# Closing the first 64 slots of each bucket before the last batch is routed, in an attention and top-2 expert kernel

## The chip, the cores and the metric

The kernel runs on one core of one Trainium2 chip. The metric is the device time of one execution in microseconds (us), as the median of several runs. The core has five engines that each execute their own list of instructions in order: TensorE (PE, matmuls and transposes), VectorE (DVE), ScalarE (ACT), GpSimd (POOL) and SyncE (SP). POOL issues the gathers, scatters and most loads, SP the writes of the token rows.

## The reference

Inputs are q, k and v (4 batches, 8 heads, 768 positions, 64 wide), 8 memory keys and values per head, and the router's and the experts' weights. First chunked attention, then a router that sends each of the 3072 tokens to two of eight experts:

```python
for c in range(nc):                       # chunks of 32, 16 to the left, 8 to the right, 8 of memory
    scores = scale * np.matmul(q_c, k_full.transpose(0, 1, 3, 2))
    a = softmax(scores)
    out[:, :, c_start:c_end] = np.matmul(a, v_full)
x = out.transpose(0, 2, 1, 3).reshape(B * S, H * D)          # 3072 tokens x 512
noisy = x @ w_gate + np.log1p(np.exp(x @ w_noise)) * noise
top2, top2_w = two largest of noisy, softmax over the two
for e in range(8):
    h = np.maximum(x[mask] @ w1[e], 0.0)                     # 512 -> 1024
    out[mask] += top2_w[mask, k, None] * (h @ w2[e])         # 1024 -> 512
```

## The kernel before

**Attention.** Work goes by 16 pairs (`NPAIR`), four for each batch. The loop of line 576 is software pipelined: in turn i, PE transposes the probabilities of pair i-1 (`PT_pe`), DVE takes the maximum over pair i's scores (`max_dve`), copies the transposed probabilities (`PT_dve`) and subtracts (`sub_dve`, whose exp runs on ACT), PE multiplies pair i-1 by the values (`PV_pe`) and forms the scores of i+1 (`scores_pe`), DVE normalizes pair i-1 into the token rows (`mult_dve`), and PE transposes rows of pair i-2 for the router (`xT_pe`, copied by ACT). The order on each engine is the order in which the program writes the calls; no scheduler changes it.

**Routing.** When the four pairs of a batch are through, `begin_route(b)` forms the logits (`logits_pe`) and the steps s1 to s8 follow, spread over the next turns by `early_steps` and `late_steps`. s1 (ACT) and s1n give noisy logits; s1m, s2d, s2a, s2g, s2b find the two largest and a one-hot of the expert pair; s3 (PE) ranks the tokens within their pair; s4 computes the gates and writes the batch's rows to `x_rows` in device memory; s5 and s5b turn ranks into a one-hot `Rn`; s4b, s6 (PE) and s7 turn that into a table `tab` of token numbers by bucket and slot. s8 (POOL) adds the batch to `seen`, the counts that s3 starts from. The last batch runs its steps on DVE (`side`), the others run some on POOL.

**Buckets.** The 28 pairs of experts are 28 buckets (`NB`) of 128 slots (`CAP`). A token beyond slot 127 of its bucket goes to a spill tile of 32. `gidx` holds the table as row numbers.

**Experts.** `gather(p)` fetches the 128 rows of bucket p by an indirect DMA from POOL. `turn(p)` transposes them on PE, and DVE copies them to `xTb`. Expert e uses seven buckets, in a larger and a smaller part (`halves(e)`): four and three. `plan[e]` lists the buckets that are new for e: seven for expert 0, six for expert 1. `first` multiplies by W1 in eight blocks of 128 outputs, each with a PSUM tile `ps_h`, followed by a ReLU on ACT or DVE. `second` multiplies one bucket by W2, and the second expert of a bucket scatters the finished rows to the output. Between the buckets of `second`, PE transposes the next expert's buckets. For expert 0, `first` is done in three pieces, and after the first of them stands `find_spill`, a chain of DVE steps that finds the tokens of the spill tile.

Between the last batch's logits and the first gather lies the whole routing chain of that batch:

```python
        begin_route(B - 1)
        late_steps()
        ...
        for p in plan[0]:
            gather(p)
        for e in range(E):
            ...
            if e == 0:
                parts = [big[:2], big[2:], small]
```

Of the kernel before, what the change touches and what calls it, by code (L numbers as in the profile page):

```python
# [24 lines left out]
def kernel(  # L25
# [35 lines left out]
    GP = 2  # L61
# [15 lines left out]
    xd_part = dram_disjoint_views(xd, B + 2)  # L77
# [7 lines left out]
    def body():  # L85
# [4 lines left out]
        psT = actx.enter_context(tc.psum_pool(name="psT", bufs=3))  # L90
# [6 lines left out]
        NVB, NKB = 3, 4  # L97
        turn_of = [0, 1, 0, 2, 1, 0, 2, 1]
        vbufs = [ap_.tile([128, ncnk, 2 * GP, 2, D], BF16, name=f"vg{i}", bufs=1) for i in range(NVB)]
# [129 lines left out]
        seen = rp.tile([128, NB], BF16, name="seen")  # L229
        rank_all = rp.tile([128, NP], F32, name="rank_all")  # L230
# [141 lines left out]
        def route(b):  # L372
# [61 lines left out]
            def s3():  # L434
# [6 lines left out]
                if b > 0:  # L441
                    nc.tensor.matmul(out=ps_r, lhsT=onesb, rhs=seen.rearrange("p (o e) -> p o e", o=1).to_broadcast([128, BT, NB]),
                                     start=False, stop=True, skip_group_check=True)
                R["ps_r"] = ps_r

            def s4():
# [4 lines left out]
                nc.vector.tensor_tensor(out=xrows[b][:, :, XC:].bitcast(F32), in0=ge, in1=bc(gs, E), op=Alu.mult)  # L451
                lo = XC if b == B - 1 else 0
                write_rows(b, b, 0, BT, lo, ROW)
# [56 lines left out]
            if b < B - 1:  # L510
                return first_steps, ((), ()), ((), (s1m, s2a, s2g, s2b, s4b)), ((s3,), (s4, s5)), ((), (s5b, s6)), ((), (s7, s8))
            return first_steps, ((), (s1n, s1m, s2d, s2a, s2g, s2b, s4b, s3, s4, s5, s5b, s6, s7))
# [62 lines left out]
        NEAR = 5  # L575
        for i in range(NPAIR):
            if i >= 1:
                PT_pe(i - 1)
            max_dve(i)
            for n in ahead(i):  # L580
                qkT_pe(n)
            fresh = i >= 3 and (i - 3) % HP == HP - 1
            if fresh:
# [4 lines left out]
            sub_dve(i)  # L588
            if i == 0:
# [12 lines left out]
            if i < NPAIR - 1:  # L602
                late_steps()
            if i in (2, 3, 4):
                zero_v(2, i - 2)
            if i >= 1:
                mult_dve(i - 1)
                if i - 1 == NPAIR - 2:
                    write_rows(B, B - 1, 0, UB, 0, XC)
            if i >= 2:  # L610
# [17 lines left out]
            if i >= 4 and i % GP == 0 and i // GP + 2 < NG:  # L628
                load_v(i // GP + 2)
            if i == GP * (NG - 3) + 1:  # L630
                load_w1(0)
                load_w2(0)
                load_w1(1)
# [4 lines left out]
        late_steps()  # L638
        PV_pe(n)
        mult_dve(n)  # L640
        write_rows(B + 1, B - 1, UB, BT, 0, XC)
        early_steps()
        xT_pe(n)
        late_steps()
# [323 lines left out]
```

## Time and profile before

| | |
|---|---|
| time, median of 3 runs | 341.07 us (340.34 to 342.45) |
| the profiled execution | 340.9 us, span 339.2 us |
| mean granted clock of PE | 0.968 |
| PE busy | 295.1 us (87%), 3492 matmuls |
| DVE busy | 170.8 us (50%), 341 instructions |
| ACT busy | 132.5 us (39%), 232 instructions |
| POOL busy | 137.9 us (41%), 181 instructions |
| indirect gathers of 128 rows | 28, mean 1061 ns on POOL |

The span is the time from the first to the last instruction of the profiled execution; its own time holds 1.7 us more around it. A busy share says how long an engine had an instruction under way, not how much of the time it set the end. In a row of the timeline stand the start and the duration in us, the engine, the line of the kernel, the operation with what it writes and reads, and in brackets the idle time before it and what ended it. A line such as L692 is a line of the kernel before.

### The profile page before, as it was taken

How to read it: one execution, taken by the hardware profiler on the slowest of the kernel's cores; microseconds unless marked ns; L12 is line 12 of the kernel's file. 1: busy time of each engine (PE TensorE's matmuls, PEld its weight loads, DVE VectorE, ACT ScalarE, POOL GpSimd, SP SyncE). 2: the span in 40 equal slices, each digit the busy share in tenths (PEclk: the TensorE clock that was granted, in tenths of full speed). 3: DMA queues.
4: the chain of work that ended last, by engine and by line, in shares of the span. 5: the costliest groups of instructions: out<-in, count | busy, mean ns of one | idle time of the engine just before them, and what ended most of it. 6: DMA issues, size and time to landing. Idle time of an engine off the chain costs nothing.

```text
span 339.2 us, 8160 instructions
## 1 busy us (share of the span) xinstructions
PE 295.1 (87%) x3492; PEld 180.0 (53%) x3492; DVE 170.8 (50%) x341; ACT 132.5 (39%) x232; POOL 137.9 (41%) x181
## 2 busy tenths in 40 slices
PE   1687888898753859999999999999999999999990
PEld 1566676776542645548547545545545545545540
DVE  7788779889686653224224233224413424434430
ACT  7867888795430423343333323223123113103100
POOL 8878885392233686400062043034250132141161
PEclk9999999999985699999999999999999999999997
DMA  7999999999991379970059129518849227221031
GB/s 102 183 180 192 187 164 198 221 104 164 228 276 26 96 111 226 224 130 2 2 84 229 31 60 198 95 56 148 181 107 200 57 80 126 40 93 53 6 130 66
DMA packets 58407, 42.87 MB, mean 126 GB/s; under 512 B 32215, under 2 KB 51799, under 8 KB 58368
## 3 DMA queue, kind: packets, MB, share of 16 engines
q0 software_dynamic: 49808, 38.80, 68.9%
q1 hardware_dynamic: 8272, 3.44, 4.7%
q8 instruction: 29, 0.48, 0.5%
q10 hardware_dynamic: 288, 0.07, 0.1%
q14 instruction: 10, 0.08, 0.1%
HBM read 61.32 MB, written 10.65 MB: 212 GB/s over the span
## 4 chain that ended last, share of the span: by engine, by line
PE 54%; issue 16%; DVE 15%; ACT 6%; POOL 5%; DMA 1%; POOLq 0%; DVEq 0%
PE ps_h L746 23%; PE ps_y L754 19%; POOL out_dram L762 4%; ACT kd L261 3%; DVE vg L136 2%; DVE mx L298 2%; DVE sd L303 2%; PE p_t L691 2%; DVE xrow L343 2%; PE ps_o L330 2%; PE ps_o L326 2%; ACT xt L356 2%; ACT P L305 1%; ACT qT L253 1%; PE ps_s L285 1%
## 5 line engine op out<-in xcount | busy, mean ns | idle before, releaser
L746 PE MATMUL ps_h<-xTb,w1t 128*128 128x512 bf16 (+3 forms) x608 | 106.6, 325 | 2.0 <-DVE xTb L692 2.0
L754 PE MATMUL ps_y<-w2t,ht 128*128 128x512 bf16 x448 | 102.0, 379 | 0.0
L746 PEld LDWEIGHTS <-w1t 128*128 128x128 bf16 x864 | 64.1, 97 | 45.2 <-DVE xTb L692 1.6
L762 POOL DMA_INDIRECT out_dram<-acc,sidx x28 | 27.9, 995 | 139.2 <-DVE acc L761 135.0
L734 DVE TENSOR_SCALAR ht<-ps_h 128x416 bf16<-128x416 f32 (+2 forms) x64 | 39.9, 625 | 72.8 <-PE ps_h L746 72.8
L732 ACT ACTIVATE ht<-ps_h 128x416 bf16<-128x416 f32 (+2 forms) x72 | 37.9, 526 | 76.7 <-PE ps_h L746 72.4
L754 PEld LDWEIGHTS <-ht 128*128 128x128 bf16 x448 | 41.9, 98 | 46.6
L758 ACT ACTIVATE acc<-ps_y,meta 128x512 f32<-128x512 f32 x28 | 19.2, 687 | 69.3 <-PE ps_y L754 56.5
L746 PE MATMUL ps_h<-xTs,w1t 128*128 128x32 bf16 x256 | 45.4, 177 | 0.2 <-DVE xTs L707 0.2
L761 DVE SCALAR_TENSOR_TENSOR acc<-ps_y,meta,acc 128x512 f32<-128x512 f32 x28 | 21.0, 751 | 37.0 <-PE ps_y L754 37.0
L682 POOL DMA_INDIRECT xl<-x_rows,gidx x28 | 29.7, 1061 | 15.4 <-issue 6.1
L120 POOL DMA_DIRECT2D vg<-in_v_dram x34 | 25.3, 753 | 8.2 <-PE ps_s L290 3.4
L692 DVE COPY xTb<-p_t 128x512 bf16<-128x512 bf16 x28 | 11.7, 422 | 29.0 <-PE p_t L691 29.0
L261 ACT COPY kd<-p_t 64x768 bf16<-64x768 bf16 x32 | 25.2, 786 | 1.0 <-PE p_t L250 0.7
L250 PE MATMUL p_t<-identb,qg 128*64 128x128 bf16 x192 | 10.3, 245 | 8.2 <-DMA qg<-in_q_dram 6.3
L305 ACT ACTIVATE P<-sd 128x768 bf16<-128x768 f32 x16 | 13.5, 844 | 9.5 <-DVE sd L303 9.5
L356 ACT COPY xt<-p_x 128x768 bf16<-128x768 bf16 x16 | 12.8, 798 | 8.0 <-PE p_x L354 7.7
L343 DVE TENSOR_TENSOR xrow<-ps_o,rec 128x768 bf16<-128x768 f32 x16 | 15.3, 958 | 0.6
L326 PE MATMUL ps_o<-memv,PT 128*128 128x260 bf16 x96 | 13.7, 279 | 2.0 <-DVE PT L317 2.0
L298 DVE TENSOR_REDUCE mx<-ps_s 128x12 f32<-128x768 f32 x16 | 15.1, 941 | 0.6 <-PE ps_s L285 0.6
L303 DVE TENSOR_TENSOR sd<-ps_s,mx 128x768 f32<-128x768 f32 x16 | 15.2, 947 | 0.0
L253 ACT COPY qT<-p_t 128x768 bf16<-128x768 bf16 x16 | 12.8, 800 | 5.0 <-PE p_t L250 4.7
(146 smaller groups left out, 305.6 us busy)
## 6 DMA issues: line engine op xcount, KB each, us to landing
w1t<-in_moe_w_dram POOLq DMA_DIRECT2D x8, 1024.0 KB
w2t<-in_moe_w_dram POOLq DMA_DIRECT2D x8, 1024.0 KB
vg<-in_v_dram POOLq DMA_DIRECT2D x30, 168.0 KB
qg<-in_q_dram POOLq DMA_DIRECT2D x7, 384.0 KB
kg<-in_k_dram POOLq DMA_DIRECT2D x7, 384.0 KB
x_rows<-xrow SPq DMA_DIRECT2D x3, 792.0 KB
x_rows<-xrow SPq DMA_DIRECT2D x2, 384.0 KB
xl<-x_rows,gidx POOLq DMA_INDIRECT x28
```

The lines of the kernel that those rows point to most:

```text
L120: nc.gpsimd.dma_start(out=vg[p0 + j:p0 + j + nj, c:c + n, hd, :, :].rearrange("p c e d -> p c (e d)"), in_=bass.AP(v.tensor, v.offset + (g ...
L261: nc.scalar.copy(st[n]["kT"][hs, hh, :].rearrange("d (p j) -> d p j", j=SJ), st[n]["p_k"][hs].rearrange("d j p -> d p j"))
L298: nc.vector.tensor_reduce(out=mx, in_=st[n]["ps"], axis=AX, op=Alu.max)
L303: nc.vector.tensor_tensor(out=sd, in0=st[n]["ps"], in1=bc4(st[n]["mx"], CTX), op=Alu.subtract)
L343: nc.vector.tensor_tensor(out=xr.rearrange("p u (h d) -> p u h d", d=D), in0=po[:, :, :MD].rearrange("p u (h d) -> p u h d", d=D), in1=rec ...
L682: nc.gpsimd.indirect_dma_start(out=xl, out_offset=None, in_=xd, in_offset=bass.IndirectOffsetOnAxis(ap=gidx[:, p:p + 1], axis=0), bounds_c ...
L732: nc.scalar.activation(out=dst, in_=src, func=Act.Relu)
L734: nc.vector.tensor_scalar(out=dst, in0=src, scalar1=0.0, scalar2=None, op0=Alu.max)
L746: nc.tensor.matmul(out=ps_h[:, o:o + w], lhsT=w1t[:, kp, f * 128:(f + 1) * 128], rhs=rhs(kp), start=(kp == 0 and i == 0), stop=(kp == KP - ...
L754: nc.tensor.matmul(out=ps_y, lhsT=ht[:, f, j * CAP:(j + 1) * CAP], rhs=w2t[:, f, :], start=(f == 0), stop=(f == FB - 1))
L761: nc.vector.scalar_tensor_tensor(out=a, in0=ps_y, scalar=gate, in1=a, op0=Alu.mult, op1=Alu.add)
L762: nc.gpsimd.indirect_dma_start(out=out_part[p], out_offset=bass.IndirectOffsetOnAxis(ap=sidx[:, p:p + 1], axis=0), in_=a, in_offset=None, ...
```

## The change

Three batches out of four are routed before attention ends. The change closes ("seals") the first 64 slots (`HB`) of each bucket to the last batch: where the three batches have filled fewer, `unsealed` raises the count from which the last batch's ranks start, so that its tokens stand in slots 64 and up. The sealed half of the buckets of experts 0 and 1 can then be fetched and multiplied by W1 while the last batch is being routed.

- Batch 2's routing is taken out of `begin_route`. Its logits stand in turn 13 (`LATE`), its steps s1m to s4 in turn 14 after `mult_dve(13)`, and s3, s8, s5, s5b, s6, s7 in turn 15, ahead of `PT_dve(15)`. Then `gidx_s` is formed from its table.
- The rows of batch 2 are written after turn 12, its gates apart.
- After the last logits POOL issues 13 gathers of 64 rows. On PE stand, in this order: half transposes of expert 0's four buckets, four blocks of its half of W1, s3 of the last batch, four more blocks, s6, the other three buckets with eight blocks, expert 1's transposes and two blocks, the overflow count, three blocks, the small matmuls of `find_spill`, three blocks.
- Then the 13 buckets are gathered again, whole, and the second half of their slots is transposed and multiplied (`turn_half(..., 1, ...)`, `half_first(e, ht, 1, ...)`).
- Steps s4b of the last batch move from POOL to DVE. `ps_h` has three buffers instead of four, `ps_y` three instead of two, the gather tiles thirteen instead of eight. The loads of W1 and W2 are issued in the order W1(0), W1(1), W2(0), over three turns.

```diff
+    HB = CAP // 2
+    SEALED = (B - 1) * S
...
                 if b > 0:
+                    before = (seen,) if b < B - 1 else (seen, unsealed)
+                    for x, r in enumerate(before):
+                        nc.tensor.matmul(out=ps_r, lhsT=onesb, rhs=r..., start=False, stop=(x == len(before) - 1), ...)
...
             def s4b():
-                eng = nc.gpsimd
+                eng = side
...
+            def s9():
+                ps_c = psT.tile([128, NB], F32, name="ps_c", tag="tr")
+                nc.tensor.matmul(out=ps_c, lhsT=onesb, rhs=seen, start=True, stop=True)
+
+            def s10():
+                short = T("short", [128, NB])
+                nc.vector.tensor_scalar(out=short, in0=R["ps_c"], scalar1=float(HB), scalar2=-1.0 / 128, op0=Alu.min, op1=Alu.mult)
+                nc.vector.tensor_scalar(out=unsealed, in0=short, scalar1=HB / 128, scalar2=None, op0=Alu.add)
...
+        NEAR, LATE = 5, HP * (B - 1) + 1
         for i in range(NPAIR):
             if i >= 1:
                 PT_pe(i - 1)
+            if i == LATE:
+                xT_pe(i - 2)
+            if i == NPAIR - 1:
+                steps["s3"]()
+                steps["s8"]()
             max_dve(i)
...
             sub_dve(i)
+            if i == NPAIR - 1:
+                steps["s5"]()
+                steps["s5b"]()
...
                 scores_pe(i + 1)
+            if i == LATE:
+                logits_pe(B - 2)
+                begin, steps = route(B - 2)
+                begin()
+            if i == NPAIR - 1:
+                steps["s6"]()
...
                 mult_dve(i - 1)
+                if i - 1 == HP * (B - 1) - 1:
+                    write_rows(0, B - 2, 0, BT, 0, XC)
                 if i - 1 == NPAIR - 2:
+                    write_rows(2, B - 1, 0, UB, 0, XC)
+                    steps["s7"]()
+                    nc.vector.tensor_scalar(out=gidx_s, in0=tabs[(B - 2) % 2][:HB], ...)
+            if i == LATE + 1:
+                for nm in ("s1m", "s2a", "s2g", "s2b", "s4b", "s4"):
+                    steps[nm]()
...
+        def turn_half(ps, h, eng):
+            p_t = psX.tile([128, KP, CAP], BF16, name="p_t")
+            hs = slice(HB * h, HB * h + HB)
+            for x, p in enumerate(ps):
+                for kp in range(KP):
+                    nc.tensor.transpose(out=p_t[:, kp, HB * x:HB * x + HB], in_=xl[hs, kp * 64:(kp + 1) * 64].bitcast(BF16), identity=identb[hs, hs])
+            ...
+            (nc.scalar.copy or nc.vector.tensor_copy)(dst, src)
...
+        for e in range(2):
+            for p in plan[e]:
+                gather_sealed(p)
+        for nm in ("s1n", "s1m", "s2d", "s2a"):
+            steps[nm]()
+        steps["s2g"]()
+        steps["s2b"]()
+        for ps in pairs(big):
+            turn_half(ps, 0, nc.scalar)
+        block = half_first(0, hts[0], 0, (0,), False, nc.scalar)
+        for f in range(4):
+            block(f)
+        steps["s3"]()
+        for nm in ("s4", "s4b", "s5", "s5b"):
+            steps[nm]()
+        for f in range(4, FB):
+            block(f)
+        steps["s6"]()
+        steps["s7"]()
...
+        for ps in pairs(small):
+            turn_half(ps, 0, nc.scalar)
+        block = half_first(0, hts[0], 0, (1,), False, nc.scalar)
+        for f in range(FB):
+            block(f)
+        for ps in pairs(plan[1]):
+            turn_half(ps, 0, nc.scalar)
+        block = half_first(1, hts[1], 0, (0, 1), False, nc.scalar)
+        block(0)
+        block(1)
         # the overflow count: 25 small matmuls
...
         for p in plan[0]:
             gather(p)
+        for f in range(2, 5):
+            block(f)
+        s_gi, s_si = find_spill()
+        gather_spill(s_gi)
+        for f in range(5, FB):
+            block(f)
...
+        for p in plan[1]:
+            gather(p)
+        load_w2(1)
         for e in range(E):
             if e == 0:
+                for x, ps in enumerate((big, small)):
+                    for pq in pairs(ps):
+                        turn_half(pq, 1, nc.vector)
+                    if x:
+                        turn_spill()
+                    block = half_first(e, ht, 1, (x,), x == 1)
+                    for f in range(FB):
+                        block(f)
+            elif e == 1:
+                block = half_first(e, ht, 1, (0, 1), True)
+                for f in range(FB):
+                    block(f)
```

`half_first` is `first` over 64 columns of each bucket instead of 128, block by block, with a ReLU of its own for the spill columns.

More of the change, by code (lines that the diff above doesn't have):

```diff
@@ L441, in s3 @@
                 if b > 0:
[L442 to L443 removed]
+                    before = (seen,) if b < B - 1 else (seen, unsealed)
+                    for x, r in enumerate(before):
+                        nc.tensor.matmul(out=ps_r, lhsT=onesb, rhs=r.rearrange("p (o e) -> p o e", o=1).to_broadcast([128, BT, NB]),
+                                         start=False, stop=(x == len(before) - 1), skip_group_check=True)
                 R["ps_r"] = ps_r
@@ L863, in body @@
             nxt = list(plan[e + 1]) if e + 1 < E else []
-            for p in nxt:
-                gather(p)
+            if e > 0:
+                for p in nxt:
+                    gather(p)
             if e + 2 < E:
```

144 lines of the change are left out of this document (92 added, 52 removed).

## The prediction

> **What bounds the kernel now.** I read the page first, then busy time in windows of 10 us, then the timeline from 63 to 136 us, where the change works, and last the chain of waits behind it.
>
> ```profile
> span 339.2 us, 8160 instructions
> ```
> ```profile
> 100.00:110.00 10.00, 2.74 (x46) 2.13 (x44) 7.21 (x35) 0.24 (x1) 3.38 (x4) 0.50 0.28 77
> 110.00:120.00 10.00, 7.05 (x56) 5.10 (x56) 6.89 (x17) 3.64 (x12) 6.85 (x7) 0.70 0.29 81
> ```
>
> Behind the times stand busy times by engine with instruction counts, PE's granted clock, DMA share and GB/s. Attention ends near 99 us. Until TensorE (PE) runs without gaps from about 127 us to the end, it mostly waits; its clock falls to 0.50 here. No DMA or other engine bounds the rest: PE's order and time do. So the change is worth what it takes from the stretch between the last attention pairs and expert 0's first W2 product, plus what it takes out of expert 1's W1 stage. Two chains of the timeline carry the rest (start, us, engine, operation, idle time before it).
>
> ```profile
> 87.48 0.23 DVE L342 RECIPROCAL rec<-ps_o 128x12 f32<-128x12 f32 x1 [1.09 <-PE ps_o L330]
> ...
> 87.75 0.96 DVE L343 TENSOR_TENSOR xrow<-ps_o,rec 128x768 bf16<-128x768 f32 x1
> ...
> 88.62 0.95 DVE L298 TENSOR_REDUCE mx<-ps_s 128x12 f32<-128x768 f32 x1
> ...
> 90.16 0.56 DVE L317 COPY PT<-p_p 128x768 bf16<-128x768 bf16 x1 [0.59 <-PE p_p L312]
> ...
> 92.46 0.23 DVE L342 RECIPROCAL rec<-ps_o 128x12 f32<-128x12 f32 x1 [0.88 <-PE ps_o L330]
> ...
> 93.60 0.55 DVE L317 COPY PT<-p_p 128x768 bf16<-128x768 bf16 x1
> ...
> 99.48 0.18 ACT L384 COPY lg<-ps_l 128x48 f32<-128x48 f32 x1
> ...
> 100.21 0.20 DVE L392 TENSOR_TENSOR nl<-ns,nz_all 128x48 f32<-128x48 f32 x1
> ...
> 101.00 0.21 DVE L401 TENSOR_TENSOR gd<-nl,m 128x48 f32<-128x48 f32 x1
> ...
> 103.13 0.27 DVE L430 TENSOR_TENSOR oh<-two 128x192 bf16<-128x192 bf16 x1
> ...
> 104.32 0.33 DVE L459 TENSOR_TENSOR rk<-oh,ps_r 128x168 f32<-128x168 bf16 x1
> ...
> 105.04 1.07 DVE L465 TENSOR_SCALAR Rn<-ramp,rank_all 128x128 bf16<-128x128 bf16 x6
> ...
> 106.66 0.18 DVE L651 TENSOR_SCALAR gidx<-tab 128x28 int32<-128x28 f32 x1
> ```
>
> VectorE (DVE) serves pairs 14 and 15 with idle gaps of 1.09, 0.59 and 0.88 us; pair 15's P transpose copy (PT) starts at 93.60. Logits of the last batch end at 99.66 (99.48 + 0.18), its routing starts at 100.21, late because DVE was still on batch 2's list, and the gather indices are there at 106.84.
>
> **Step 1: batch 2's routing moves ahead of pair 15.** DVE executes in order. Its list s1m, s2a, s2b, s4 now stands between mult(13) and max(15), and s5, s5b between sub(15) and mult(14), with s7 and gidx_s before PT(15). The same lists for batch 1:
>
> ```profile
> 72.19 0.19 DVE L399 TENSOR_REDUCE m<-nl 128x6 f32<-128x48 f32 x1
> ...
> 73.84 0.23 DVE L342 RECIPROCAL rec<-ps_o 128x12 f32<-128x12 f32 x1
> ...
> 77.17 0.20 DVE L448 TENSOR_TENSOR ge<-ge,two 128x48 f32<-128x48 f32 x1
> ...
> 77.99 0.32 DVE L459 TENSOR_TENSOR rk<-oh,ps_r 128x168 f32<-128x168 bf16 x1
> ```
>
> First list: 73.84 - 72.19 = 1.65, and 77.99 - 77.17 = 0.82, together 2.47 us; max(15) goes from 88.62 to 91.1. From max(15) to PT(15) there were 4.98 us with 0.59 + 0.88 idle, so 3.51 of work. The idle goes: pair 14's products need 1.74 us after its PT (90.72 to 92.46) and DVE has sub(15) and the second list meanwhile. Second list, rk to the end of Rn: 106.11 - 104.32 = 1.79. Two more of 0.2 each (gidx's row). PT(15) starts at 91.1 + 3.51 + 1.79 + 0.4 = 96.8 instead of 93.60: **3.2 us late**. Queued behind it are PV(15), mult(15), the last transposes and logits: 6.06 us from PT(15) to 99.66 before, so logits end at 102.86. Routing starts then, 2.7 later than now, since DVE is free. Bounds: if the 1.09 gap fills too, 2.1 late; if none fills, 4.7.
>
> **Step 2: the sealed gathers on GpSimd (POOL).** 13 gathers of 64 rows start 0.6 us after gidx_s (106.84 to 107.45 now), at 97.4. No such gather is in the trace.
>
> ```profile
> 6.47 0.58 POOL L120 DMA_DIRECT2D vg<-in_v_dram  x1
> ...
> 107.45 1.18 POOL L682 DMA_INDIRECT xl<-x_rows,gidx  x1 [2.82 <-DVE ov L790]
> ...
> 110.51 0.61 PE L691 MATMUL p_t<-identb,xl 128*128 128x128 bf16 x4 [2.42 <-DMA xl<-x_rows,gidx]
> ...
> 112.93 1.65 POOL L682 DMA_INDIRECT xl<-x_rows,gidx  x1 [0.30 <-issue]
> ```
>
> Bounds for one: 0.58, a plain DMA of 20 short rows, and 1.65, the slowest 128-row gather, plus 0.30 between two. I take 0.8 + 0.3, between the plain one and the usual 1.01. Thirteen end at 111.7; the first data land 3.05 after issue (110.50 - 107.45), the thirteenth at 113.7. The 13 full gathers, the spill gather and three weight loads queue behind them.
>
> **Step 3: what PE puts ahead of batch 3's ranks.** s3, the rank matmuls, now stand behind two half transposes and four blocks of expert 0. The first copy out of PSUM on ScalarE (ACT) stands behind the exp that needs gd.
>
> ```profile
> 112.89 5.14 PE L746 MATMUL ps_h<-xTb,w1t 128*128 128x256 bf16 x32 [0.52 <-DVE xTb L692]
> ...
> 116.32 2.13 ACT L732 ACTIVATE ht<-ps_h 128x256 bf16<-128x256 f32 x5 [0.29 <-PE ps_h L746]
> ...
> 118.11 0.62 PE L691 MATMUL p_t<-identb,xl 128*128 128x128 bf16 x8
> ...
> 120.17 3.67 PE L746 MATMUL ps_h<-xTb,w1t 128*128 128x256 bf16 x32 [1.44 <-DVE xTb L692]
> ```
> ```profile
> L356 ACT COPY xt<-p_x 128x768 bf16<-128x768 bf16 x16 | 12.8, 798 | 8.0 <-PE p_x L354 7.7
> ...
> L732 ACT ACTIVATE ht<-ps_h 128x256 bf16<-128x256 f32 x12 | 4.6, 383 | 7.1 <-PE ps_h L746 6.9
> ...
> L692 DVE COPY xTb<-p_t 128x512 bf16<-128x512 bf16 x28 | 11.7, 422 | 29.0 <-PE p_t L691 29.0
> ```
>
> gd ends 1.0 after routing starts (101.21 - 100.21): 103.9; the exp, like lg's 0.18, ends at 104.1. A copy of 512 columns on ACT lies between 0.38 (256) and 0.80 (768): 0.59. Copy, transposes at the low clock (0.61), copy: blocks start at 106. At the low clock, four blocks take 3.3 us (relu four starts at 116.32, PE began at 112.89), at the full clock 4 x 0.46. PE has been almost idle since 102.9, so I take 3.3: 109.3. s3 0.5 (0.92 now, with other DVE work between): 109.8, where DVE had its input ready at 106.1. Ranks and Rn 1.79, then 0.73 to the indices (106.84 - 106.11): **112.4, 5.6 later than now**. Blocks four to seven run under Rn; PE passes s6 at 112.0. If the clock stays up, 1.4 less.
>
> **Step 4: PE's order up to expert 0's W2.** One p_t buffer serves all half transposes, so each pair costs transposes (0.4, half the row of eight), copy and 0.1 of hand-over: 1.08 on ACT, 0.92 on DVE (0.42). Pair and single of the small half: 1.8. Eight blocks of 192 columns at ACT's 0.38: 3.0. Three pairs of expert 1: 3.25. PE is at 120.05.
>
> ```profile
> 85.20 0.74 PE L365 MATMUL ps_l<-wgn,xt 128*128 128x16 bf16 x24 [0.55 <-ACT xt L356]
> ...
> 108.82 0.18 DVE L800 TENSOR_TENSOR srank<-srank,ps_s 128x24 f32<-128x24 f32 x1 [1.10 <-PE ps_s L797]
> ...
> 109.22 0.15 DVE L807 CAST partb<-part 128x1 bf16<-128x1 f32 x1
> ...
> 112.75 0.95 DVE L812 TENSOR_TENSOR sone<-ramp,srank 128x768 bf16<-128x768 bf16 x1
> ...
> 115.96 1.44 DVE L818 TENSOR_REDUCE sum<-where 128x32 bf16<-128x768 bf16 x1
> ```
> ```profile
> 127.27 5.99 PE ps_h L746 x63
> 133.26 1.74 PE ps_y L754 x8
> 135.00 0.22 PE p_t L691 x4
> ...
> 147.37 12.98 PE ps_h L746 x128
> ```
>
> A matmul of 512 columns takes 0.217 (1.74 / 8), the smallest 0.031 (0.74 / 24). An expert 1 half block has 256, 128 and 64 columns four times: 0.77. Two blocks: 121.6; the overflow count, 25 tiny ones, 0.8: 122.4. DVE then needs 0.55 (108.82 to 109.37) and 4.65 for the spill search (112.75 to 117.40): 127.6. PE's three blocks under it end at 124.7, so **PE stands 2.9 us**, in order, although the full gathers have landed. Three more blocks: 130.1. Then expert 0's second halves: two pairs 1.85, 3.67, small half and spill transposes 2.25, last blocks 32 x (0.081 + 0.025) = 3.4 (0.025 for the 32 columns: 5.99 / 32 less 384 columns). W2 of expert 0 starts at 141.3; now 133.26: **+8.0**.
>
> **Step 5: what comes back.** Expert 1's W1 stage is 12.98 now; with half its columns left it takes 32 x (0.193 + 0.025) = 7.0: **-6.0**. Six sets of four transposes between W2 products get 64 columns each, 0.22 to 0.12: -0.6. Four ps_h buffers become three: relus of 0.38 hide under the next block, so nothing; at worst one per expert shows, 8 x 0.38 = 3.0. The later experts do the same work. The second gather of 13 buckets moves rows twice but lands ten us before PE asks.
>
> Edits at nothing, with their cover: logits(2) and its ACT steps move up one pair, behind scores(14), and take PE's 0.74 before PT(13) instead of after it, with xT(11) gone ahead. Batch 2's row write leaves SP one pair after its last mult, some 15 us before the first sealed gather waits for it; its gates follow alone. The three weight loads keep their place behind batch 1's POOL steps. The matmul and two DVE ops for unsealed run while PE and ACT make the last logits. oht and ohp, on DVE now, stand before the rank multiply, which waits for s3 until 109.8 anyway; without that cover about 0.5. The spill columns' own relus, 16 small ones on DVE, run beside ACT's.
>
> Sum: 8.0 - 6.0 - 0.6 = **+1.4 us**. The profiled execution took 340.9 (span 339.2 and 1.7 around it), so 342.3; the median of the runs shown, 341.07, is 0.2 above it. That is no change within the 1% (3.4 us) that a measurement of this kernel can tell from nothing. I sum by where PE can go on, since the added work fits the idle time of 100 to 120 us, but its order, not its load, decides.
>
> **Rivals.**
> - *Starved gathers (slower).* One gather beside DVE's 0.95 us sone took 1.65 instead of 1.01. If DVE's routing lists do that to all sealed gathers, the pitch is 1.95: the thirteenth starts at 97.4 + 12 x 1.95 = 120.8 and lands at 123.9, where its transposes are due at 119.0: 4.9 later, 347.2. It decides from a pitch of 1.54. Against it: gathers beside other DVE work took 1.01 to 1.18.
> The Trainium skill, page "SBUF — State Buffer", section "Who interferes with whom", says that VectorE copies and tensor_scalars in a two-port mode keep GpSimd from writing descriptors until they end, but infers that tensor_tensor does not. The slow gather here stood beside a tensor_tensor, so the measurement goes further than the page; by the page alone only PT and Rn (0.55 and 1.07) would stall gathers, too little for this rival, and 342.3 stands.
> - *PE's load decides (faster).* If PE really never waits after its first block, its work from 106 (3.3 + 0.5 + 1.8 + 0.4 + 2.6 + 6.2 + 1.0 + 3.7 + 3.4 and about 3 of transposes) ends at 132: 9.3 less, 333.0. For it: the windows show PE 73% idle at 100 to 110. Against it: one p_t buffer and the spill search in PE's order.
> - *DVE's gaps take batch 2's lists whole (no change).* Routing starts as now: 2.7 less, 339.6. Against it: 4.66 us of lists against gaps of 2.56, one of which waits on PE still.
> - *The clock stays up (no change).* 340.9. Against it: it stands at 0.50 over all of 100 to 110 us, where PE is 27% busy.
>
> **Chances.** Forecast 0.48, own range 339.5 to 345.5, of which 0.12 above 344.5; starved 0.20; load 0.12; gaps 0.10; clock 0.10. Faster by over 1%: 0.12. Slower: 0.20 + 0.12 = 0.32. Within 1%: 0.56. The range runs from 338.0 (gaps and clock together, 338.2) to 347.5 (starved); it leaves out the load case and little else.
>
> **What would show it.** Right: max(15) starts some 2.5 us later, with no DVE idle before PT(15); rank matmuls start about 3 us after oh; PE waits about 3 us before the eight tiny spill matmuls; expert 1's W1 stage takes near 7. Wrong: sealed gathers at a pitch over 1.5; PE without a wait before the spill matmuls; logits ending before 101; the low clock absent at the first sealed block; expert 0's W2 starting before 137 or after 145.

## Result and the profile after

The changed kernel takes 353.98 us, the kernel before 341.76 beside it: a ratio of 1.034 (95% interval 1.028 to 1.041). Two later measurements of the same pair gave 1.042 (1.036 to 1.047, and 1.037 to 1.047), so 11 to 14 us are lost where I had forecast 342.3 and no change. One of the four executions here (358.78 us), two of `change_again` (358.1 and 360.69) and two of `route_first_again` (356.67 and 357.03) were slow ones at a lower granted clock; times in this document are medians of all executions, and without these the three medians are 353.2, 353.6 and 351.2 us. The profiled execution took 353.15 us.

The page's first row and the windows that answer to those of before:

```profile
span 351.2 us, 8581 instructions
```
```profile
100.00:110.00 10.00, 4.94 (x83) 3.87 (x81) 5.54 (x16) 3.18 (x7) 3.10 (x3) 0.84 0.57 138
110.00:120.00 10.00, 7.08 (x54) 5.38 (x53) 3.06 (x15) 3.69 (x9) 7.56 (x9) 0.59 0.27 57
```

PE's busy time from 100 to 120 us has only gone from 9.8 to 12.0: the idle stretch that the sealed rows were to fill is filled little, and it lasts longer. The timeline shows where each station of the prediction now lies, behind one row of the kernel before, its maximum of pair 14:

```profile
84.02 0.95 DVE L298 TENSOR_REDUCE mx<-ps_s 128x12 f32<-128x768 f32 x1
```

```profile
87.40 0.96 DVE L302 TENSOR_REDUCE mx<-ps_s 128x12 f32<-128x768 f32 x1 [0.45 <-PE ps_s L289]
...
92.16 0.19 DVE L403 TENSOR_REDUCE m<-nl 128x6 f32<-128x48 f32 x1
...
95.17 0.95 DVE L302 TENSOR_REDUCE mx<-ps_s 128x12 f32<-128x768 f32 x1
95.28 0.36 SPq L463 DMA_DIRECT2D x_rows<-gt  x1
...
98.05 1.48 PE L334 MATMUL ps_o<-vg,PT 128*32 128x256 bf16 x24
...
100.95 0.17 DVE L646 TENSOR_SCALAR gidx_s<-tab 64x28 int32<-64x28 f32 x1
101.28 0.56 DVE L321 COPY PT<-p_p 128x768 bf16<-128x768 bf16 x1 [0.16 <-PE p_p L316]
...
106.29 1.11 POOL L713 DMA_INDIRECT xl<-x_rows,gidx_s  x1 [9.29 <-issue]
...
107.17 0.18 ACT L388 COPY lg<-ps_l 128x48 f32<-128x48 f32 x1
...
109.70 0.39 PE L724 MATMUL p_t<-identb,xl 64*128 64x64 bf16 x4 [3.02 <-DMA xl<-x_rows,gidx_s]
...
114.18 3.57 PE L807 MATMUL ps_h<-xTb,w1t 128*128 128x256 bf16 x16 [0.67 <-ACT xTb L731]
...
118.48 0.33 DVE L469 TENSOR_TENSOR rk<-oh,ps_r 128x168 f32<-128x168 bf16 x1 [6.73 <-PE ps_r L448]
...
120.86 0.18 DVE L893 TENSOR_SCALAR gidx<-tab 128x28 int32<-128x28 f32 x1
```

Pair 14's maximum, ahead of anything that the change moved on DVE except one pair's logits, is already 3.4 us late (84.02 before). The sealed indices are ready at 101.12, yet the first sealed gather starts at 106.29. PE then waits for its rows. The chain of waits names what the gather waited for, and shows the rest (start, us, what):

```profile
95.28 9.97 DMA x_rows<-gt
...
132.27 0.87 DVE sone L930
133.16 0.96 DVE where L932
134.12 2.69 DVE sum L936 x2
137.05 2.44 PE ps_h L807 x36
...
150.70 1.67 PE ps_y L836 x7
152.37 0.22 PE p_t L724 x4
152.59 1.83 PE ps_y L836 x8
...
172.55 1.46 PE ps_y L836 x6
```

W2 of expert 0 starts at 150.70 instead of 133.26, 17.4 us late. The write of batch 2's gates, 24 KB, takes 9.97 us to land. It stands in SP's queue behind the write of batch 2's rows: the records of single transfers in the trace have its first piece at 100.51, and the rows, issued at 82.67, land at 103.64.

### The profile page after: what moved, and what is told of

It reads as the page before. It is cut to its first block, busy times and chain, and to the rows that moved or that the text cites. A ratio compares the mean times of both kernels' runs of the same rounds, so it can differ in the third digit from the quotient of the medians.

```text
span 351.2 us, 8581 instructions
## 1 busy us (share of the span) xinstructions
PE 300.6 (86%) x3656; PEld 188.6 (54%) x3674; DVE 166.0 (47%) x347; ACT 143.8 (41%) x259; POOL 149.3 (43%) x192
## 4 chain that ended last, share of the span: by engine, by line
PE 66%; DVE 13%; ACT 7%; issue 6%; DMA 4%; POOL 2%; POOLq 0%; DVEq 0%
PE ps_y L836 25%; PE ps_h L828 22%; PE ps_h L807 7%; DMA x_rows<-gt 3%; ACT kd L265 2%; DVE vg L139 2%; PE ps_o L334 2%; DVE mx L302 2%; PE ps_o L330 2%; DVE xrow L347 2%; DVE sd L307 2%; POOL out_dram L844 2%; ACT xt L360 1%; PE p_t L724 1%; PE p_t L254 1%
## 5 line engine op out<-in xcount | busy, mean ns | idle before, releaser
L836 PE MATMUL ps_y<-w2t,ht 128*128 128x512 bf16 x430 | 99.9, 379 | 1.6 <-issue 1.0
L828 PE MATMUL ps_h<-xTb,w1t 128*128 128x512 bf16 (+3 forms) x416 | 78.4, 336 | 0.0
L788 ACT ACTIVATE ht<-ps_h 128x512 bf16<-128x512 f32 (+4 forms) x92 | 45.4, 493 | 75.2 <-PE ps_h L828 54.9
L790 DVE TENSOR_SCALAR ht<-ps_h 128x512 bf16<-128x512 f32 (+3 forms) x68 | 35.6, 523 | 68.6 <-PE ps_h L828 55.7
L828 PEld LDWEIGHTS <-w1t 128*128 128x128 bf16 x608 | 44.4, 96 | 34.7
L828 PE MATMUL ps_h<-xTs,w1t 128*128 128x32 bf16 x192 | 34.1, 177 | 0.0
L807 PE MATMUL ps_h<-xTb,w1t 128*128 128x128 bf16 (+3 forms) x320 | 31.0, 254 | 2.1 <-ACT xTb L731 1.6
L807 PEld LDWEIGHTS <-w1t 128*128 128x128 bf16 x320 | 26.2, 102 | 5.7 <-issue 2.0
L713 POOL DMA_INDIRECT xl<-x_rows,gidx_s x13 | 12.9, 990 | 12.9 <-issue 12.6
L330 PE MATMUL ps_o<-memv,PT 128*128 128x260 bf16 x96 | 14.7, 293 | 3.2 <-DVE PT L321 3.2
```

The source lines that it names most:

```text
L330: nc.tensor.matmul(out=po[:, u, :OW], lhsT=PT[:, 2 * u + e, :], rhs=memv[:, g, e, :], start=(e == 0), stop=False, skip_group_check=True)
L788: nc.scalar.activation(out=dst, in_=src, func=Act.Relu)
L790: nc.vector.tensor_scalar(out=dst, in0=src, scalar1=0.0, scalar2=None, op0=Alu.max)
L807: nc.tensor.matmul(out=ps_h[:, o:o + w], lhsT=lhsT, rhs=xTv[:, kp, z[0]:z[-1] + 1:(z[1] - z[0] if len(z) > 1 else 1), hs], start=(kp == 0 ...
L828: nc.tensor.matmul(out=ps_h[:, o:o + w], lhsT=w1t[:, kp, f * 128:(f + 1) * 128], rhs=rhs(kp), start=(kp == 0 and i == 0), stop=(kp == KP - ...
L836: nc.tensor.matmul(out=ps_y, lhsT=ht[:, f, j * CAP:(j + 1) * CAP], rhs=w2t[:, f, :], start=(f == 0), stop=(f == FB - 1))
```

## The experiments

They ran in five groups, each on one chip with the kernel before beside it, which took 344.3, 342.4, 342.6, 341.2 and 341.4 us. I compare within a group, or by ratio. The diffs are shortened, and where the order is all that changes, they name steps instead of quoting every line.

**1. Four single edits, in a bad moment.** `late_gates` issues batch 2's gate write behind the sealed gathers:

```diff
-                    nc.sync.dma_start(out=xd_part[b - (B - 2)]..., in_=gt.bitcast(I32))   # in s4
+        gate_rows(0, B - 2, late_gates)                    # behind the 13 gather_sealed
```

> Edit: the gate write of batch 2 is issued behind the sealed gathers instead of ahead of them (the gate columns of its rows hold zeros until then; no sealed gather's gate columns are used). Theory 1 (the first sealed gather waits 4.6 us for this write to land, 106.29 against gidx_s at 101.12): the first sealed gather starts some 0.6 us after gidx_s, at about 101.7; no transpose of a sealed row waits for a gather any more, the first four cold blocks start at about 111 instead of 114.2, W2 of expert 0 at about 147 instead of 150.7, and the time is 349 to 350.5 us, 3 to 4.5 below the change. Rival A (the weights' traffic starves the gathers themselves): they are issued at 101.7, but their pitch goes from 1.27 us to over 1.8 and they land later than 5 us after issue while the weights arrive; the blocks start no earlier than 113 and the time stays above 352. Rival B (PE is held by something else there): the gathers are early, the blocks still start at 114, no gain.

`w2_later`:

```diff
-            if i == GP * (NG - 3) + 2:
-                load_w2(0)
+        load_w2(0)                                         # behind the 13 gather_sealed
```

> Edit: W2 of expert 0 (1 MB) is loaded behind the sealed gathers instead of at turn 12. Theory 1a (the gate write's 768 pieces of 32 bytes need 9.97 us because they stand behind 3 MB of weights and the rows, which arrive at 240 GB/s until about 102): 1 MB less is some 4.4 us less, the write lands at about 101, the first sealed gather starts within 1 us of gidx_s, and the time falls by 3 to 4.5 us against the change, as in the run beside it. Rival C (the write takes 10 us by itself, its pieces are small): it lands some 10 us after its issue as before, the first sealed gather starts at about 106, and the time stays at 352 to 354. In both, W2 of expert 0 lands by about 130, ahead of its first use at about 147.

`route_first`:

```diff
+        steps["s3"](); s4, s4b, s5, s5b
         for f in range(4):
             block(f)
-        steps["s3"](); s4, s4b, s5, s5b
+        steps["s6"]()
         for f in range(4, FB):
             block(f)
-        steps["s6"]()
```

> Edit: the last batch's rank matmuls go to PE ahead of the four cold blocks and its index matmuls behind them (the change has them 4 and 8 blocks later). Theory 2 (the indices' lateness, 120.9 against 106.7 before, is not what sets the end: POOL is busy with sealed gathers until 122.8 and the first full gather's rows are used at 139.5): gidx comes 3 to 4 us earlier, the first full gather stays at about 123, PE's wait ahead of the spill sums falls by 0 to 1 us, the time stays within 1 us of the change (352.2 to 354). Rival D (the ranks and the indices are on the path, as the term of 5.6 us in the sum has it): the spill search and W2 of expert 0 come 3 us earlier, the time falls to about 350.

`early_search`:

```diff
+        overflow count; for p in plan[0]: gather(p)       # right behind gidx
         small half: turn_half, eight blocks; turn_half(expert 1)
+        s_gi, s_si = find_spill(); gather_spill(s_gi)
         block = half_first(1, hts[1], 0, (0, 1), False, nc.scalar)
```

> Edit: the overflow count is put right behind the last indices, and the spill search ahead of expert 1's first block (the change has them behind two and five of its blocks). Theory 3 (PE stands about 3 us ahead of the spill sums, waiting for DVE's list of 5.2 us behind the overflow count): that wait goes, expert 1's blocks run through, W2 of expert 0 starts at about 147.7 instead of 150.7, the time is 350 to 351. Rival E (something else ends that wait, the full gathers or the spill's gather): the second halves of expert 0 wait for rows instead, W2 of expert 0 stays after 149.5 and the time above 352.

Measured: 379.7, 378.1, 375.9 and 381.1 us, ratios 1.105, 1.095, 1.093 and 1.105, all 22 to 27 us longer than the change. Their traces hold stands that nothing explains, as ACT's second sealed copy in `route_first`, 4.6 us after its transposes had ended:

```profile
110.31 0.39 PE L724 MATMUL p_t<-identb,xl 64*128 64x64 bf16 x4 [0.45 <-DMA xl<-x_rows,gidx_s]
...
115.30 0.59 ACT L731 COPY xTb<-p_t 128x512 bf16<-128x512 bf16 x1 [5.86 <-remote]
```

So the times decide nothing yet; two rows do. In `late_gates` the gate write is out of the way and the first gather is still late, and in `w2_later` it is on time (one fence each):

```profile
103.99 0.17 DVE L653 TENSOR_SCALAR gidx_s<-tab 64x28 int32<-64x28 f32 x1
...
108.31 1.11 POOL L721 DMA_INDIRECT xl<-x_rows,gidx_s  x1 [8.28 <-DVE unsealed L532]
```
```profile
101.45 0.17 DVE L646 TENSOR_SCALAR gidx_s<-tab 64x28 int32<-64x28 f32 x1
...
102.06 1.10 POOL L711 DMA_INDIRECT xl<-x_rows,gidx_s  x1 [4.57 <-DVE gidx_s L646]
```

The name in the first bracket only ended close to the gather's start; the gather doesn't need it, since in `aligned_w2_later` below it starts 4 us ahead of `unsealed`. The gather's own waits in the program are three row writes, the gate write, an older load and the index. In `late_gates` the rows of batch 2 were issued at 84.48 and landed at 107.36, 0.95 us ahead of the gather. So not the gate write alone: the rows, issued some 20 us ahead of the index, are late too as long as 3 MB of weights are under way. `w2_later` needs no gate edit to be on time. Two things remained open: the stands, and what made attention late.

**2. The change again, and two edits.** `change_again` and `before_again` are the two kernels unchanged; the latter, run once, took 340.7 us.

> The changed kernel once more, unaltered, beside the edits of this call: in the first four runs each edit gave 373 to 380 us where the change had been 353, with DVE, ACT and PE standing 2.4 to 6.5 us at a time between 107 and 171 us for nothing that a row of theirs names. Theory F (these stands are a delivery of instructions or descriptors that comes late while many small transfers run, and vary with the chip or the moment): the change itself comes out at 370 to 380 here, with the same stands. Rival G (each of the four edits brought them on): the change stays at 352 to 355 and stands nowhere over 1.5 us in that stretch.

`gates_and_search` has the edits of `late_gates` and `early_search` together; `expert0_only` leaves expert 1's sealed gathers, transposes and eight blocks out of the stretch, and expert 1 runs its W1 whole, as before:

```diff
-        for e in range(2):
-            for p in plan[e]:
-                gather_sealed(p)
+        for p in plan[0]:
+            gather_sealed(p)
...
-            elif e == 1:
-                half_first(e, ht, 1, (0, 1), True), eight blocks
```

> Edit: both the gate write of batch 2 behind the sealed gathers and the spill search ahead of expert 1's blocks. Theories 1 and 3 (4.6 us of wait for the gate write, 3 us of PE's wait ahead of the spill sums, both on the path): 5 to 7.5 us below the change in the same call. Rival (other stands take their place): less than 2 us below it.

> Edit: only expert 0's buckets are gathered sealed and multiplied ahead; expert 1's six sealed gathers, its turns and its eight blocks ahead are gone and it is treated as the experts behind it. Theory 4 (expert 1's 11 us ahead, 128.3 to 139.5 with the wait in it, and 3.2 of turns cost more than the 6 us that its stage saves): W2 of expert 0 starts 8 us earlier than in the change, expert 1's W1 stage is 13 instead of 7, the time is 1 to 3 us below the change in the same call. With theory F on top, fewer small transfers are fewer stands: up to 10 us below it. Rival H (PE stood idle anyway until the full gathers have landed, so that the work ahead of expert 1 is free): 4 to 6 us above the change.

Measured: 356.6 (1.042), 370.4 (1.081) and 355.6 us (1.040, interval 1.037 to 1.044). No stands this time, and the change repeats.

`gates_and_search` has a flaw of mine, the same as `early_search`: the full gathers stand in POOL's order ahead of transposes that I had left behind them, and these now read the full gathers' rows. Its timeline:

```profile
125.73 0.95 SPq L557 DMA_DIRECT2D x_rows<-gt  x2
...
129.04 1.04 POOL L745 DMA_INDIRECT xl<-x_rows,gidx  x1 [5.13 <-DMA x_rows<-gt]
...
137.22 0.39 PE L732 MATMUL p_t<-identb,xl 64*128 64x64 bf16 x4 [12.89 <-DMA xl<-x_rows,gidx]
```

So both kernels say nothing on the search. The first row does say something: batch 2's gate write, the first of its two, issued at 125.73 when no weights move, has landed at 127.70 by the trace, 2.0 us later, not 9.97. `expert0_only` reaches W2 of expert 0 at 145.90, 3.8 us earlier than `change_again` (149.74) where I had expected 8, and pays it back with 12.98 us of W1 for expert 1, where the change needs 7.0. Expert 1's share of the change is worth nothing that these times can tell.

**3. Places of the tiles.** The change adds small tiles ahead of `qg`, `kg`, `vg` and the weights, which moves all of them 832 bytes on, from a multiple of 256 to one plus 64. `before_shifted` does that to the kernel before, with an unused tile; `aligned` takes it back in the change:

```diff
     wp = ctx.enter_context(tc.tile_pool(name="wp", bufs=1))
+    filler = rt.tile([128, 16], F32, name="filler", bufs=1)     # before_shifted: 64 bytes
+    filler = rt.tile([128, 48], F32, name="filler", bufs=1)     # aligned: 192 bytes
```

> Edit: the kernel before with 64 bytes of filler at that place, nothing else: its tiles now lie as the change's do, 64 bytes behind a multiple of 256. Theory 5: 256-byte pieces take 44 ns and over, the maximum of turn 14 comes at 86 to 87.5 instead of 84.0 to 84.6, the time is 2 to 4 us above the kernel before. Rival J: 41 to 42 ns, no difference beyond 1 us.

> Edit: the change with 192 bytes of filler per partition ahead of the weights' tiles, nothing else. In the kernel before, the tiles of the weights and of the q, k and v loads began at addresses that are multiples of 256 bytes; the change's new small tiles and buffer counts push all of them 832 bytes on, to 64 behind such a multiple, and the filler takes them to a multiple again. In the transfer records the 256-byte pieces of those loads take 41 ns in the kernel before and 44 to 59 ns in the change and every edit of it. Theory 5 (that shift slows the loads of the attention stage, PE's instructions come later behind them, 1.0 to 1.2 us at turns 8 and 9): 256-byte pieces back at 41 to 42 ns, the maximum of turn 14 at 84.0 to 84.8 instead of 86.7 to 87.4, and the time 2 to 3.5 us below the change (349 to 352 where it has 353 to 356). Rival J (the pieces are slow for another reason, the order of the v buffers or the traffic of that chip): 44 ns and over, turn 14 at 86 or later, no gain.

`aligned_w2_later` adds the edit of `w2_later`; `aligned_w2_search` adds to that the early search with the full gathers behind all sealed transposes:

> Edit: the filler, and W2 of expert 0 loaded behind the sealed gathers. Theory 1a (with 1 MB less ahead of them, the rows and gates of batch 2 have landed when the sealed indices are ready): the first sealed gather starts 0.6 us after gidx_s, the first four cold blocks start at 109 to 110 with the gather landing some 2.6 us after issue, W2 of expert 0 at 143 to 144, and the time is 4 to 5.5 us below the filler alone. Rival (PE then waits elsewhere): less than 2 us below it. In the first run with this edit the stage from 107 to 160 held stands of 2 to 10 us that no row explains; should they be here too, they belong to the tiles' place or to that edit, and not to the moment.

> Edit: as the run before, and the spill search ahead of expert 1's blocks, its first part right behind the last indices (this time the full gathers stay behind the turns of the sealed rows; in the two earlier runs with this edit the turns of the three buckets of the small half read the full gathers' rows and PE waited 12.9 us for them). Theory 3: PE's wait of about 2.5 us ahead of the spill sums goes, W2 of expert 0 starts 2.5 to 3 us earlier than in the run before, at about 141, the time is 2 to 3 us below it, near the kernel before. Rival E: another wait takes its place, less than 1 us.

Measured: `before_shifted` 344.12, ratio 1.0046 (1.0006 to 1.0087); `aligned` 352.71, 1.030 (1.020 to 1.039); `aligned_w2_later` 348.89, 1.016 (1.009 to 1.024); `aligned_w2_search` 347.63, 1.013 (1.006 to 1.020).

An unused tile of 64 bytes costs the kernel before 1.6 us; the interval allows 0.2 to 3.0, and I had expected 2 to 4. The profile shows how: the DMA part of the pages of `before_again` and of `before_shifted` have the same packets and bytes in the queue of loads, at another share of the time,

```profile
q0 software_dynamic: 49808, 38.80, 69.0%
```
```profile
q0 software_dynamic: 49808, 38.80, 72.2%
```

and turn 14's maximum, with the longest stand of PE ahead of it, in the timelines of the two:

```profile
84.61 0.95 DVE L298 TENSOR_REDUCE mx<-ps_s 128x12 f32<-128x768 f32 x1
```
```profile
56.88 0.50 PE L286 MATMUL ps_s<-kd,qT 128*32 128x112 bf16 x20 [2.19 <-issue]
...
87.41 0.95 DVE L299 TENSOR_REDUCE mx<-ps_s 128x12 f32<-128x768 f32 x1
```

Over all profiled executions this maximum starts at 84.0 to 86.7 in the eight with aligned tiles (median 84.8), at 85.8 to 91.5 in the twelve with shifted ones (median 88.3). Three of the eight stand at 86.3 to 86.7, so the place of the tiles is not all that moves it. The records of single transfers separate the two without an overlap: 21,492 pieces of 256 bytes take 41.3 to 41.5 ns on average in the eight, 45.4 to 54.2 in the twelve. The median piece takes 41 in all; 0.4 to 0.6% against 5 to 13% take over 80. For the change itself the time alone doesn't separate it: the interval of `aligned` overlaps the change's.

The weights are the larger part. W2 of expert 0 moved behind the gathers is worth 3.8 us beside `aligned`, with all four executions of the one below all four of the other. DMA in windows of 2 us (last column GB/s), first of `aligned`, whose index was ready at 98.20 and whose first gather started at 103.31, then of `aligned_w2_later`, 100.08 and 100.36:

```profile
98.00:100.00 2.00, 1.63 (x32) 1.38 (x36) 0.63 (x3) 1.12 (x2) 0.00 (x0) 1.00 1.22 237
100.00:102.00 2.00, 0.77 (x22) 0.47 (x12) 1.46 (x4) 0.00 (x0) 0.00 (x0) 1.00 0.55 135
```
```profile
98.00:100.00 2.00, 2.00 (x36) 1.59 (x26) 1.48 (x5) 0.41 (x1) 0.00 (x0) 0.50 0.00 0
100.00:102.00 2.00, 1.75 (x14) 1.26 (x12) 0.63 (x2) 1.11 (x2) 1.33 (x2) 0.61 0.55 197
```

The traces also hold when each write landed, which the gather waits for (us):

| | change | `late_gates` | `aligned` | `aligned_w2_later` |
|---|---|---|---|---|
| rows of batch 2, issued | 82.67 | 84.48 | 80.67 | 82.54 |
| rows of batch 2, landed | 103.64 | 107.36 | 100.80 | 98.09 |
| gates of batch 2, landed | 105.25 | behind the gathers | 102.27 | 98.55 |
| last piece of W2 of expert 0 | 104.5 | 108.6 | 101.5 | behind the gathers |
| sealed index ready | 101.12 | 104.16 | 98.20 | 100.08 |
| first sealed gather | 106.29 | 108.31 | 103.31 | 100.36 |

With W2 ahead of the gathers, the writes land about when it does, and the gather starts 0.95 to 1.04 us behind the last of them; with W2 behind the gathers, both writes are there before the index. The gather doesn't wait for the load itself: in `late_gates` it starts before W2's last piece. The search ahead of expert 1's blocks gains 1.3 us, less than the 2.5 us that PE had stood there, and inside the intervals. In `aligned_w2_search` another wait shows: the transposes of the second pair wait for the first copy on ACT, which stands behind the last batch's exp.

```profile
107.25 0.59 ACT L730 COPY xTb<-p_t 128x512 bf16<-128x512 bf16 x1
...
107.89 0.37 PE L723 MATMUL p_t<-identb,xl 64*128 64x64 bf16 x4 [2.26 <-ACT xTb L730]
```

**4. What is left, aligned.** All three start from `aligned_w2_search` or its parts. `sealed_copy_first` puts the first copy ahead of the exp:

```diff
-        for nm in ("s1n", "s1m", "s2d", "s2a"): ...
+        for nm in ("s1n", "s1m", "s2d"): ...
+        turn_half(pairs(big)[0], 0, nc.scalar)
+        s2a, s2g, s2b
```

> Edit: on top of the filler, the later W2 load and the early spill search, ACT's first copy of sealed rows goes ahead of the last batch's exponential (L423 there), nothing else. Theory 6 (with the gathers early, the first transposes end at 105.6 and their copy stands on ACT until 107.25 behind that exponential, which waits for the routing list on DVE; PE waits 2.26 us for the copy's buffer): the copy starts at about 105.7, PE's wait falls below 0.8, the first blocks start at 108.3 to 108.8 instead of 109.7, the time is 1 to 1.5 us below aligned_w2_search. Rival K (the third and fourth gathers land no earlier, 108.6): the blocks start at 109.3 or later, less than 0.5 us.

`route_first_aligned` adds the edit of `route_first` to `aligned_w2_search`, `expert0_only_aligned` that of `expert0_only` to `aligned_w2_later`; `change_third` is the change.

> Edit: on top of the filler, the later W2 load and the early spill search, the last batch's rank and index matmuls go 4 and 8 blocks ahead as in route_first. Theory 2: the indices come 3 us earlier, the first full gather stays behind POOL's sealed gathers at about 117.5, the time stays within 1 us of aligned_w2_search (347.6). Rival D: 2 us or more below it. If stands of 2 us and more that no row explains appear between 107 and 160 us, as in route_first, they go with this edit; if not, they went with that moment.

> Edit: the filler and the later W2 load, and expert 1's sealed gathers, turns and eight blocks ahead left out as in expert0_only. Theory 4, corrected by that run (W2 of expert 0 came 3.8 us earlier there though its attention stage had been 2.3 us slower, and expert 1's stage took 13 instead of 7): what expert 1's work costs ahead, 6 us, is what it saves behind, so the time is within 1.5 us of aligned_w2_later (348.9). Rival H: 4 to 6 us above it. Rival L (less low clock and fewer transfers make it the better kernel): 2 us or more below it.

Measured: 346.07 (1.015, 1.011 to 1.019), 346.25 (1.012, 1.005 to 1.019), 347.92 (1.020, 1.014 to 1.026), and the change 355.11 beside them. In the change's profile of this group the index comes at 103.28, the gates land at 104.59 and the first sealed gather starts at 105.63, 2.3 us behind the index where I had expected 4.5 to 5.3. The repairs of `sealed_copy_first` together give 9.0 us of the change's 13.9 back. PE's wait for the first copy falls to 0.96:

```profile
105.50 0.27 PE L723 MATMUL p_t<-identb,xl 64*128 64x64 bf16 x4 [0.96 <-ACT xTb L730]
...
108.55 3.57 PE L806 MATMUL ps_h<-xTb,w1t 128*128 128x256 bf16 x16 [0.67 <-ACT xTb L730]
```

The wait for the next rows grows to 1.71, so part of the gain goes there. The three kernels lie within 1.9 us of each other, so the copy, the place of the rank matmuls and expert 1's early half can't be told apart by the time. None beats the kernel before.

**5. Two of the first group again.**

> The edit of w2_later once more (W2 of expert 0 behind the sealed gathers, tiles where the change has them). If the stands of 2.4 to 10.6 us on ACT, DVE and PE in its first run belonged to the moment: none over 1.5 us after 100 us, the first sealed gather 0.5 us behind gidx_s, the time 3 to 5 us below the change's 353 to 356, so 349 to 352. If they belong to the edit: 370 and over with the same stands.

> The edit of route_first once more (the last batch's rank and index matmuls 4 and 8 blocks ahead, tiles where the change has them). Moment: no stands, 352 to 356, within 1.5 us of the change. Edit: 370 and over, ACT at the second sealed copy and at the first block's result 4 to 6 us late again.

`w2_later` takes 351.17 (1.025, 1.017 to 1.033, where the change had 1.034 to 1.042) instead of 378.1, `route_first` 354.37 (1.026, 1.017 to 1.036) instead of 375.9. So the 22 to 27 us of the first group belonged to its moment, not to these two edits; the other two were not run again alone. The interval of `route_first` overlaps the change's, so its edit can't be told from none. The chip alone did not bring the stands either, since the second group ran on the same one and the change had no such stands there. The kernel before took 344.3 beside them. What the stands were stays open.

## Why the prediction was wrong

The prediction's way, leg by leg, in the profiled executions (us; `repaired` is `sealed_copy_first`):

| | before | predicted | change | repaired |
|---|---|---|---|---|
| maximum of pair 14 starts | 84.02 | 84.02 | 87.40 | 84.64 |
| logits of the last batch end | 99.66 | 102.86 | 107.35 | 104.88 |
| first sealed blocks start | | 106 | 114.18 | 108.55 |
| indices of the last batch | 106.84 | 112.4 | 121.04 | 115.8 |
| spill sums end | | 127.6 | 137.05 | 123.8 |
| W2 of expert 0 starts | 133.26 | 141.3 | 150.70 | 142.97 |
| span | 339.2 | 340.6 | 351.2 | 343.5 |

9.4 of the 10.6 us by which the span misses the forecast are there at W2 of expert 0. By the prediction's steps:

- *A step that I didn't have (3.4 us here, 3.5 between the medians).* "Edits at nothing" went through what the change issues, not through where it puts its tiles. Pair 14's maximum is late before any moved step reaches it but batch 2's logits; `aligned` moves that pair's logits too, and has its maximum at 84.87. Shifted by 64 bytes, the kernel before loses 2.8 us at the same place. That the small pieces are slower is shown; that this delay reaches PE through late instructions ("issue") fits its stands, but is only argued.
- *The failed step: "Edits at nothing", the row write (2 to 5 us).* I had the sealed gathers at 97.4, waiting for nothing but their index, as the rows left "some 15 us before". They left then, at 82.67; they landed at 103.64, and the gates behind them at 105.25, about when the weights had. From the index (101.12) to the gather (106.29) it takes 5.2 us, in the change's two other profiles 4.4 and 2.3, in `aligned_w2_later` 0.3. The trace of the kernel before had shown the price: batch 1's rows, issued at 78.10 beside weight loads, landed at 91.92, 13.8 us later, and in the change batch 2's rows stand behind such a write. The first blocks went from 4.5 us late at the logits to 8.2 late; with W2 loaded behind the gathers, the time gains 3.8.
- *Step 1, right in kind, 1.1 us short.* From maximum 14 to maximum 15 it takes 7.77 us against 4.60: 3.17 of lists where I had 2.5. PT(15) starts at 101.28, 7.7 late; less the 3.4 of maximum 14 that is 4.3, where I had 3.2 and 4.7 as the bound. PV(14) has its share in it: its two parts take 1.48 us each, with the clock granted 0.50 from 96 to 100 us, where pair 13's took 0.84 and 0.85, and DVE waits 0.45 us for them. These 1.1 us are there at the logits too.
- *Step 2, pitch.* 0.96 + 0.30 = 1.26 instead of 1.1: thirteen gathers take 16.5 us, not 14.3. PE waits for the first four only, which start within 4.2 us where I had 3.3. The rival of starved gathers has fallen: its pitch was 1.95, and the gather beside Rn (119.33, Rn from 119.20) took 0.96 like the others.
- *Step 3.* Blocks at the low clock 3.57 for four (3.3 predicted). ACT's exp ahead of the first copy was named there; where the rows are on time, it makes PE wait 1.3 us longer (2.26 against 0.96).
- *Step 4, right.* PE stands 1.35 + 1.15 = 2.5 us before the spill sums (2.9 predicted):

```profile
135.52 0.19 PE L940 MATMUL ps_s<-partb,sum 128*32 128x1 bf16 x4 [1.35 <-DVE sum L936]
136.86 0.19 PE L940 MATMUL ps_s<-onesb,sum 128*32 128x1 bf16 x4 [1.15 <-DVE sum L936]
```

- *Step 5, half right.* Expert 1's W1 stage takes 7.0, as worked out: -6.0. The half transposes between W2's products take 0.22 for four, as the full ones, and the product behind takes 1.83 instead of 1.73. So +0.5 instead of -0.6; the chain row `152.37 0.22 PE p_t L724 x4` above shows it.

In the repaired kernel, W2 of expert 0 starts 1.7 us behind the forecast, although the search and the copy are early there, and 1.2 more are lost behind it, by Step 5. Its profiled execution took 345.43. So with the tiles and the loads in place the forecast was still 3 us too low, and the change a loss of 1.5% (1.1 to 1.9): none of the rivals, the price of several steps that were each a little short.

## What to carry to other kernels

A new tile is an edit too: before costing a change, compare the addresses of the large tiles before and after, and hold those that small pieces are loaded into on a multiple of 256 bytes (64 bytes behind one is the only other place that was run here). A gather that reads rows through memory can't start before their writes have landed, and that took 21 us here beside the weights: look in the profile at what such a write already takes and at the GB/s in the windows ahead of the gather, and hold loads that nobody needs yet behind it. And filling an idle stretch pays only if the work that is put in isn't itself in the order ahead of what ends the stretch.

## What the runs showed of the hardware

- *Places of tiles.* The aligned and shifted pieces above: 41.4 against 45 to 54 ns on average. The Trainium skill, page "DMA: Bandwidth & Descriptors", section "How a descriptor splits into AXI transactions", says that a transaction must start from an address that is a multiple of 256, and that the bytes ahead of an unaligned start are fetched for nothing. An estimate by that: every shifted piece of 256 bytes would cost 10 beats of 32 bytes instead of 8. The runs agree in direction only: the median piece is as fast as before, the loss is in the 5 to 13% that take over 80 ns; and the page speaks of reads, where here it is the written side that is shifted.
- *A gather's price.* 64 rows take POOL 0.96 us, 128 rows 1.01: twice the rows cost 0.05 more.
- *Half transposes.* Four of 64x64 take PE 0.22, as long as four of 128x128.
- *Small writes behind loads.* 24 KB of gates land 9.97 us after issue behind the rows and beside weights at some 240 GB/s, 2.0 us after it alone. A row write of 792 KB took 13.8 us beside the loads in the kernel before, and one issued at 98.10, as they ended, 5.5 us.
- *Open.* The stands of the first group (2.4 to 10.6 us on ACT, DVE and PE); the granted clock between 95 and 130 us, from 0.50 to 1.00 by stretches that differed between executions, which no run varied.
